# A two-layer attention and feed-forward kernel: the opening rebuilt, more doubled score matmuls, and another rule for the order of TensorE's last work

## The chip, the cores and the metric

The kernel runs on one core of one Trainium2 chip. The metric is the device time of one execution in microseconds. Every run is also profiled, and the "span" in a profile is the time from the first to the last instruction.

TensorE does the matmuls, ScalarE the exponentials, VectorE and GpSimd the rest; SyncE issues the transfers. PSUM is the memory that this kernel's matmuls write to, and an eviction is a copy out of it. The granted clock is the share of full speed at which the profile shows TensorE running. A warm-up or filler matmul is one whose result nobody reads.

## The reference

Two layers, each attention followed by a feed-forward block, both with a residual and a layer norm without gain. There are 2048 rows of 448 columns, 16 heads of 28, and a hidden width of 1792.

```python
x = A_x
x = x + attention(layernorm(x), wqkv, wo)      # softmax(q k^T / sqrt(28)) v, 16 heads
x = x + mlp(layernorm(x), w1, b1, w2, b2)      # relu(x w1 + b1)^2 w2 + b2
x = x + attention(layernorm(x), wqkv, wo)
x = x + mlp(layernorm(x), w1, b1, w2, b2)
```

## The kernel before

The kernel is a program that plans itself. While it is built, a planner keeps one clock per engine, takes the next operation from several streams (scores, exponentials, attention values, loads, one chain per block of rows) and emits it on its engine in that order. On the chip each engine then runs its own list in order.

Scores are computed transposed, three "units" of 128 keys by 512 columns to a group (32-row matmuls, four heads packed). One ScalarE exponential of 1536 columns turns a group into weights. Some units are set aside: VectorE computes their exponential by a polynomial.

```python
# every priority stream offers its next operation; the earliest start wins
s, _, e, st = min(cands, key=lambda c: (c[0], c[1]))
```

```python
# the opening: unread warm-up matmuls, emitted before anything else of TensorE
idle = ps_m[0].tile([P, QB], DT.float32, name="mt", tag="m")
for _ in range(WARM):                                  # 34
    nc.tensor.matmul(idle[:, 0:D], lhsT=b2w[:, 0:P], rhs=b2w[:, :], start=True, stop=True)
...
# loads: both halves of the first rows, then query/key weights, then value weights
yield dma(x_sb[:, 0:2, :], x_view[:, 0:2, :], 224 * kb, ("x", 0, 0))
yield dma(x_sb[:, 2:4, :], x_view[:, 2:4, :], 224 * kb, ("x", 0, 1))
yield dma(st_qk[:, 0:3, :], qk_main, 680 * kb, ("wqk", 0))
...
# the first passes take keys in four parts of 512; one pass is 4 heads of one query block
add_passes(0, [0, 1], [0, 4, 8, 12, 16])
```

```python
# doubled scores: a group is computed once or twice more in front, into the same PSUM, when TensorE
# has been busy for less than HOT of the last HWIN us and there is room before the last exponential ends
short = HOT - pl.load(HWIN) if s_left else 0.0         # HOT = 0.8
again = 0
if short > 0 and gi > 0:
    last = ("e" in gbuf[gi - 1] and gbuf[gi - 1]["e"].end) or pl.clock["ACT"] + 1.35
    again = max(0, min(MORE, int(min(o.room, last - LAT["PE"] - o.end) / 0.22)))
```

The softmax here doesn't subtract the row's maximum and nothing guards it: scores larger than these inputs give would overflow.

Of the kernel before, what the change touches and what calls it, by code (L numbers as in the profile page):

```python
# [11 lines left out]
DT = mybir.dt  # L12
AF = mybir.ActivationFunctionType
ALU = mybir.AluOpType
P = 128
H = 16
# [11 lines left out]
WARM = 34  # L28
GATE = [None, None, ('Q', 0, 0, 0), ('Q', 0, 0, 0), ('Q', 0, 2, 0), ('Q', 0, 2, 0), ('Q', 0, 2, 0), ('Q', 0, 2, 0)]
# [17 lines left out]
HOT = 0.8  # L47
# [44 lines left out]
class Planner:  # L92
# [3 lines left out]
    def __init__(self):  # L96
        self.clock = {"PE": 0.0, "ACT": 0.0, "DVE": 0.0, "POOL": 0.0, "DMA": 0.0, "-": 0.0}
        self.mode = None
        self.tok = {}
        self.streams = []  # L100
        self.past = {"PE": [], "DVE": []}

# [35 lines left out]
    def run(self):  # L138
        while self.streams:
# [14 lines left out]
            s, _, e, st = min(cands, key=lambda c: (c[0], c[1]))  # L154
# [29 lines left out]
def kernel(  # L184
# [78 lines left out]
    def dma(out_ap, in_ap, nbytes, key):  # L263
        return Op("DMA", nbytes / 230e3, lambda e: nc.sync.dma_start(out=out_ap, in_=in_ap), sets=key)

    def setup():
# [13 lines left out]
        nc.gpsimd.memset(V_sb[0][:, :, :, DH:DHP], 1.0)  # L280
        nc.gpsimd.memzero(wo[:])
        nc.gpsimd.memset(w1[DL:P, 3, :], 0.0)

        idle = ps_m[0].tile([P, QB], DT.float32, name="mt", tag="m")
        for _ in range(WARM):
            nc.tensor.matmul(idle[:, 0:D], lhsT=b2w[:, 0:P], rhs=b2w[:, :], start=True, stop=True)  # L286

    def late_setup():

        yield Op("POOL", 0.2, lambda e: nc.gpsimd.memset(sel[:], 0.0), deps=[("K", 0, 1, 3)])  # L290
# [13 lines left out]
    def loads():  # L304
        kb = 1024
        yield dma(x_sb[:, 0:2, :], x_view[:, 0:2, :], 224 * kb, ("x", 0, 0))
        yield dma(x_sb[:, 2:4, :], x_view[:, 2:4, :], 224 * kb, ("x", 0, 1))
        qk_main = A_wqkv[0:3 * P, 0:2 * D].rearrange("(c p) n -> p c n", p=P)
        yield dma(st_qk[:, 0:3, :], qk_main, 680 * kb, ("wqk", 0))
        yield dma(st_qk[0:DL, 3, :], A_wqkv[3 * P:D, 0:2 * D], 112 * kb, ("wqk",))  # L310
        v_main = A_wqkv[0:3 * P, 2 * D:3 * D].rearrange("(c p) n -> p c n", p=P)
# [6 lines left out]
        for hh in range(G):  # L318
            yield dma(wo[DHP * hh:DHP * hh + DH, :, :],
                      A_wo.rearrange("(g hh r) d -> hh r g d", hh=G, r=DH)[hh], 98 * kb, ("wo", hh))  # L320
        yield dma(w1[:, 0:3, :], B_w1[0:3 * P, :].rearrange("(c p) n -> p c n", p=P), 1344 * kb, ("w1", 0))
# [5 lines left out]
    def wprep():  # L327
# [9 lines left out]
        yield Op("ACT", 0.6, cp(wk, D, 0, 4), deps=[("wqk",)], sets=("wk", 0))  # L337
        yield Op("ACT", 0.6, cp(wq, 0, 0, 4), deps=[("wqk",)], sets=("wq", 0))
        yield Op("ACT", 1.3, cp(wk, D, 4, H), deps=[("wqk",)], sets=[("wk", g) for g in range(1, G)])
        yield Op("ACT", 1.3, cp(wq, 0, 4, H), deps=[("wqk",)], sets=[("wq", g) for g in range(1, G)])  # L340
# [27 lines left out]
    s_left = [True]  # L368

# [14 lines left out]
    def layernorm(t0, nt, deps_of, early=False, mv=None):  # L384
# [14 lines left out]
        rs = Op("POOL", 0.6, rsqrt, deps=[last])  # L399
# [11 lines left out]
        def turn(p0, own, xs):  # L411
# [17 lines left out]
            o = Op("DVE" if early else engs_now(), 0.12 + 0.3 * len(xs), ev, deps=[t], rel=t)  # L429
# [4 lines left out]
        for p0 in range(0, nt, 2):  # L434
# [4 lines left out]
            for j in js:  # L439
# [6 lines left out]
                nm = Op("DVE", 0.42, norm, deps=[rs])  # L446
# [40 lines left out]
    def copy_to(dst, by=None):  # L487
        def f(e, t):
            src = t[:, :] if len(dst.shape) == 2 else t[:, :].rearrange("p (r n) -> p r n", r=dst.shape[1])
# [10 lines left out]
    def qkv(l, t0, nt, xnT, own_xt, ends, early=False):  # L500
# [4 lines left out]
        def turned(w, dst, key, wkey, g0):  # L505
# [5 lines left out]
                copy_to(d, q_scale if key == "Q" else None), 0.70, [*ends, *[(wkey, g) for g in range(g0, g0 + r)]], True,  # L511
# [17 lines left out]
        ks = [(wk, K_sb[l], "K", "wk", g) for g in range(0, G, r)]  # L529
        qs = [(wq, Q_sb, "Q", "wq", g) for g in range(0, G, r)]  # L530
        if l == 0 and t0 == 0:
            yield from turned(*ks[0])
            yield from turned(*qs[0])
            yield from values()
            for a, b in zip(ks[1:], qs[1:]):
                yield from turned(*a)
                yield from turned(*b)
            yield Op("DVE", 0.0, None, deps=[last], rel=own_xt)
        else:
            yield from turned(*ks[0])  # L540
            yield from values()
            for a in ks[1:]:
# [454 lines left out]
```

## Time and profile before

| | before |
|---|---|
| time, median of 11 runs of one batch | 934.02 us |
| span of the profiled run | 934.9 us |
| ScalarE busy | 96%, 890.3 us of it 662 exponentials |
| first exponential starts | 15.44 us |
| waits before exponentials after 26 us | 5.46 us |
| from the end of the last exponential to the end | 21.3 us |

A line of the timeline gives start, length, engine, source line, operation, what it writes from what, and in brackets the idle time in front and who ended it. A line of the stretches gives its borders and length, the busy time of TensorE, its weight loads, VectorE, ScalarE and GpSimd with instruction counts, then the granted TensorE clock, the DMA share and GB/s. The prediction shows the main lines. Here are four stretches of one us that it does not show, where the clock falls for the first time:

```profile
99.00:100.00 1.00, 0.05 (x6) 0.01 (x3) 0.16 (x1) 1.00 (x2) 0.00 (x0) 1.00 0.00 0
100.00:101.00 1.00, 0.87 (x8) 0.30 (x8) 0.00 (x0) 1.00 (x2) 0.00 (x0) 1.00 0.00 0
101.00:102.00 1.00, 0.67 (x22) 0.46 (x24) 0.00 (x0) 1.00 (x2) 0.00 (x0) 1.00 0.00 0
102.00:103.00 1.00, 1.00 (x22) 0.41 (x14) 0.89 (x2) 1.00 (x2) 0.00 (x0) 0.55 0.00 0
```

TensorE was busy 1.59 of the 3 us before the fall (0.05 + 0.87 + 0.67), and its longest pause in them was 0.95 us. So here the clock fell without a pause of even one us.

### The profile page before, as it was taken

Reading aid. Unit: us, or ns where it says so; the run is one execution under the profiler, and the core shown is the slowest. Engines: PE = TensorE matmul, PEld = TensorE weight load, DVE = VectorE, ACT = ScalarE, POOL = GpSimd, SP = SyncE. Lnnn points to the kernel's source line nnn. Section 1 sums busy time; section 2 is a strip of 40 time slices with the busy share of each in tenths; the row PEclk is TensorE's granted clock in tenths of the full one; section 3 lists DMA queues with packets and bytes.
Section 4 is the critical chain, followed back from the end, with each engine's and each line's share of the span. In section 5 each row is a group of like instructions: output and inputs, shape, how many; then the busy total and the mean of one; then the engine's idle time right before and its main releaser. Section 6 shows DMA issues by size and latency. Waiting matters only on the chain.

```text
span 934.9 us, 28645 instructions
## 1 busy us (share of the span) xinstructions
PE 825.9 (88%) x12718; PEld 447.8 (48%) x12718; DVE 633.1 (68%) x1323; ACT 900.8 (96%) x678; POOL 41.5 (4%) x84
## 2 busy tenths in 40 slices
PE   8999878999889899999988998788989887989886
PEld 4555434454444445444454544434445444555554
DVE  6755576677776778767767656767667576576673
ACT  5999999999999999999999999999999999999992
POOL 4100000000000000000000000000000000000000
PEclk9999898999899999999999999999999999999998
DMA  9000010000000000000000000011000000000000
GB/s 274 13 2 1 2 38 19 14 9 13 14 9 13 14 8 13 13 12 4 2 2 2 1 2 2 9 37 31 24 15 16 24 17 14 20 17 24 20 11 11
DMA packets 34472, 18.40 MB, mean 20 GB/s; under 512 B 18474, under 2 KB 33899, under 8 KB 34348
## 3 DMA queue, kind: packets, MB, share of 16 engines
q1 hardware_dynamic: 34348, 16.58, 6.4%
q8 instruction: 99, 1.62, 0.7%
q14 instruction: 25, 0.20, 0.1%
HBM read 14.26 MB, written 2.07 MB: 17 GB/s over the span
## 4 chain that ended last, share of the span: by engine, by line
ACT 69%; issue 17%; PE 10%; DMA 2%; DVE 1%; SPq 0%; POOLq 0%; POOL 0%; ACTq 0%
ACT pt L668 69%; PE sc L650 3%; PE mt L476 3%; DMA dn<-oT_sb 2%; PE oT L771 1%; PE sc L476 1%; PE mt L286 1%; PE mt L951 1%; PE tp L417 0%; DVE vh L703 0%; DVE st L378 0%; DVE x_sb L866 0%; DVE oT_sb L796 0%; DVE vi L681 0%; DVE dn L838 0%
## 5 line engine op out<-in xcount | busy, mean ns | idle before, releaser
L668 ACT ACTIVATE pt<-sc 128x1536 bf16<-128x1536 f32 x662 | 890.3, 1739 | 6.3 <-PE sc L650 4.9
L650 PE MATMUL sc<-Q_sb,K_sb 32*128 32x256 bf16 (+1 forms) x5194 | 292.3, 264 | 88.7 <-ACT pt L668 84.1
L650 PEld LDWEIGHTS <-K_sb 32*128 32x128 bf16 x5361 | 131.5, 93 | 265.2 <-issue 255.3
L771 PE MATMUL oT<-pt,V_sb 128*32 128x256 bf16 (+1 forms) x4468 | 153.6, 266 | 0.6 <-ACT pt L668 0.6
L476 PE MATMUL mt<-xnT,w 128*128 128x256 bf16 (+1 forms) x968 | 122.8, 265 | 5.2 <-DVE vi L681 1.6
L771 PEld LDWEIGHTS <-V_sb 128*32 128x32 bf16 x4608 | 94.6, 97 | 45.4 <-issue 40.8
L904 DVE TENSOR_SCALAR r<-mt 128x512 bf16<-128x512 f32 x110 | 74.6, 678 | 47.1 <-PE mt L476 46.3
L476 PEld LDWEIGHTS <-w 128*128 128x128 bf16 x1008 | 82.3, 100 | 40.4 <-issue 31.4
L703 DVE SCALAR_TENSOR_TENSOR vh<-vh,vm 128x512 f32<-128x512 f32 x126 | 86.2, 684 | 1.7
L681 DVE TENSOR_SCALAR vi<-mt 128x512 int32<-128x512 f32 x63 | 43.4, 689 | 51.5 <-PE mt L650 51.1
L866 DVE TENSOR_TENSOR x_sb<-x_sb,mt 128x448 bf16<-128x448 bf16 x62 | 38.0, 613 | 40.3 <-PE mt L476 39.9
L951 PE MATMUL mt<-xn,ident 128*128 128x448 bf16 x187 | 63.1, 369 | 1.6 <-DVE xn L443 0.9
L476 PE MATMUL mt<-w,h 128*128 128x448 bf16 x224 | 53.1, 355 | 0.0
L476 PE MATMUL mt<-w,V_sb 128*128 128x448 bf16 x210 | 48.8, 354 | 0.0
L397 POOL TENSOR_TENSOR ve<-mv,eps_t 128x2 f32<-128x2 f32 (+1 forms) x34 | 9.6, 281 | 873.9 <-DVE mv L379 792.9
L708 DVE SCALAR_TENSOR_TENSOR pd<-vh,vi 128x512 bf16<-128x512 f32 x63 | 43.1, 685 | 1.7 <-PE oT L771 0.9
L703 DVE SCALAR_TENSOR_TENSOR vh<-vm 128x512 f32<-128x512 f32 x63 | 43.0, 682 | 0.0
L378 DVE BATCH_NORM_STATS2 st<-x_sb 128x6 f32<-128x448 bf16 x64 | 39.4, 616 | 1.2 <-DMA x_sb<-in_A_x_dram 0.6
L794 DVE COPY oT_sb<-oT 128x256 f32<-128x256 f32 (+1 forms) x52 | 19.7, 380 | 28.7 <-PE oT L771 28.1
L476 PE MATMUL mt<-xnT,wk 128*128 128x256 bf16 x240 | 33.1, 274 | 1.3 <-DVE V_sb L523 0.8
L443 DVE TENSOR_SCALAR xn<-x_sb,mv,rstd 128x448 bf16<-128x448 bf16 x64 | 23.5, 391 | 14.5 <-POOL rstd L398 14.1
L476 PE MATMUL mt<-xnT,wq 128*128 128x256 bf16 x240 | 33.1, 274 | 0.1
(78 smaller groups left out, 636.1 us busy)
## 6 DMA issues: line engine op xcount, KB each, us to landing
rec<-scr SPq DMA_DIRECT2D x52, 128.0 KB
x_sb<-in_A_x_dram SPq DMA_DIRECT2D x8, 224.0 KB
out_dram<-x_sb SPq DMA_DIRECT2D x16, 112.0 KB
w<-in_B_w_dram SPq DMA_DIRECT2D x1, 1568.0 KB
w<-in_B_w_dram SPq DMA_DIRECT2D x1, 1344.0 KB
dn<-oT_sb SPq DMA_DIRECT2D x52, 4.0 KB
scr<-dn SPq DMA_DIRECT2D x52, 4.0 KB
rec<-scr SPq DMA_DIRECT2D x12, 64.0 KB
```

Source lines behind the costliest of these rows:

```text
L378: nc.vector.bn_stats(out=st[:, :], in_=x_sb[:, t0 + j, :])
L443: nc.vector.tensor_scalar(out=xn[:, 0:D], in0=x_sb[:, t0 + j, :], scalar1=mv[0][:, j, 0:1], scalar2=ln["r"][:, j:j + 1], op0=ALU.subtract, ...
L476: nc.tensor.matmul(box["t"][:, c0:c0 + n], lhsT=lhsT() if callable(lhsT) else lhsT, rhs=rhs, start=a, stop=b)
L650: nc.tensor.matmul(dst[k][:, i * nt * P:(i + 1) * nt * P], lhsT=K_sb[l][rows, g, (kb + i) * P:(kb + i + 1) * P], rhs=Q_sb[rows, g, t0 * P: ...
L668: nc.scalar.activation(out=pt[:, 0:n], in_=gbuf[gi]["sc"][:, 0:n], func=AF.Exp, scale=float(np.log(2.0)) * 2.0 ** -23)
L681: nc.vector.tensor_scalar(out=box["i"][:, :], in0=src, scalar1=EXP_BIAS, scalar2=0.0, op0=ALU.add, op1=ALU.max)
L703: nc.vector.scalar_tensor_tensor(out=h[:, :], in0=src, scalar=b, in1=m, op0=ALU.add, op1=ALU.mult)
L708: nc.vector.scalar_tensor_tensor(out=pd[:, :], in0=h[:, :], scalar=b0, in1=i.bitcast(DT.float32), op0=ALU.add, op1=ALU.mult)
L771: nc.tensor.matmul(box["t"][DHP * hh:DHP * hh + DHP, 0:n], lhsT=V_sb[l][:, kb + i, 4 * g + hh, :], rhs=p[:, c0:c0 + n], start=begin and kb ...
L866: nc.vector.tensor_tensor(out=x_sb[:, tb, :], in0=x_sb[:, tb, :], in1=t[:, 0:D], op=ALU.add)
L904: nc.vector.tensor_scalar(out=r[:, 0:w], in0=t[:, 0:w], scalar1=0.0, scalar2=None, op0=ALU.max)
L951: nc.tensor.matmul(t[:, 0:D], lhsT=ident[:, :], rhs=xns[0][:, 0:D], start=True, stop=True)
```

## The change

The intent: start the stream of exponentials earlier, keep TensorE's clock up by more doubled scores, spend unread matmuls only in idle time, and let TensorE's last work go by readiness. The core of the diff, with cuts marked:

```diff
-WARM = 34
+COLD = 7.0
...
+CUT0 = (0, 2, 4, 8, 12, 16)
...
-HOT = 0.8
+HOT = 0.9
...
-            s, _, e, st = min(cands, key=lambda c: (c[0], c[1]))
+            s, _, e, st = min(cands, key=lambda c: (max(c[3][2].ready, self.clock[c[2]]) if c[2] == "PE" and self.turns() else c[0], c[1]))
...                                       # turns() is true once no scores are left to emit
+    def warm_up():                       # a stream of the lowest priority, until wk of group 0 is there
...
-        yield dma(x_sb[:, 2:4, :], x_view[:, 2:4, :], 224 * kb, ("x", 0, 1))
         yield dma(st_qk[:, 0:3, :], qk_main, 680 * kb, ("wqk", 0))
         yield dma(st_qk[0:DL, 3, :], A_wqkv[3 * P:D, 0:2 * D], 112 * kb, ("wqk",))
+        yield dma(x_sb[:, 2:4, :], x_view[:, 2:4, :], 224 * kb, ("x", 0, 1))
...                                       # wq is spread by VectorE, wk by ScalarE; three buffers are
...                                       # zeroed after the first statistics; values come last in block 0
+        gs = [(0, 1), (1, 1), (2, 2)] if early and ONE else [(g, r) for g in range(0, G, r)]
...
-    add_passes(0, [0, 1], [0, 4, 8, 12, 16])
+    for cut in zip(CUT0, CUT0[1:]):
+        if cut == (0, 2):
+            add_passes(0, [0], cut)      # first block's keys alone, first query block
+        elif cut == (2, 4):
+            add_passes(0, [0], cut)
+            add_passes(0, [1], (0, 4))
+        else:
+            add_passes(0, [0, 1], cut)
```

More of the change, by code (lines that the diff above doesn't have):

```diff
@@ L27 @@
 EXP_POLY = (37.74184817, 23.12456889, 12.30728893, -0.14556782)
-WARM = 34
-GATE = [None, None, ('Q', 0, 0, 0), ('Q', 0, 0, 0), ('Q', 0, 2, 0), ('Q', 0, 2, 0), ('Q', 0, 2, 0), ('Q', 0, 2, 0)]
+COLD = 7.0
+WQD = 1
+TURNS = 1
+ENDU = 100
+HOTE = 0.8
+WSTOP = ('wk', 0)
+XT = 1
+VEND = 1
+CUT0 = (0, 2, 4, 8, 12, 16)
+ONE = 1
+GATE = [None, None, ('Q', 0, 0, 0), ('Q', 0, 0, 0), ('s', 8), ('s', 8), ('s', 8), ('s', 8)]
 EARLY = 2
@@ L101, in __init__ @@
         self.past = {"PE": [], "DVE": []}
+        self.turns = lambda: False
     def load(self, span, eng="PE"):
@@ L261, with dma @@
     mhalf = const.tile([P, 4], DT.float32, name="mhalf")
-    def dma(out_ap, in_ap, nbytes, key):
-        return Op("DMA", nbytes / 230e3, lambda e: nc.sync.dma_start(out=out_ap, in_=in_ap), sets=key)
+    def dma(out_ap, in_ap, nbytes, key, deps=()):
+        return Op("DMA", nbytes / 230e3, lambda e: nc.sync.dma_start(out=out_ap, in_=in_ap), sets=key, deps=deps)
     def setup():
@@ L279, in setup, with junk @@
             nc.vector.memset(t[:, D:D + 1], 1.0)
-        nc.gpsimd.memset(V_sb[0][:, :, :, DH:DHP], 1.0)
-        nc.gpsimd.memzero(wo[:])
-        nc.gpsimd.memset(w1[DL:P, 3, :], 0.0)
-        idle = ps_m[0].tile([P, QB], DT.float32, name="mt", tag="m")
-        for _ in range(WARM):
-            nc.tensor.matmul(idle[:, 0:D], lhsT=b2w[:, 0:P], rhs=b2w[:, :], start=True, stop=True)
+    def warm_up():
+        box = {}
+        def junk(e):
+            if "t" not in box:
+                box["t"] = bank(first, "mt")
+            nc.tensor.matmul(box["t"][:, 0:D], lhsT=b2w[:, 0:P], rhs=b2w[:, :], start=True, stop=True)
+        first = o = Op("PE", 0.38, junk, acq=R_m)
+        yield o
+        while pl.tok.get(WSTOP) is None or pl.tok[WSTOP].end > pl.clock["PE"]:
+            o = Op("PE", 0.38 if pl.clock["PE"] < COLD else 0.19, junk)
+            yield o
+        yield Op("PE", 0.0, None, deps=[o], rel=first)
     def late_setup():
+        yield Op("POOL", 1.0, lambda e: nc.gpsimd.memset(V_sb[0][:, :, :, DH:DHP], 1.0), deps=[("rs", 2)])
+        yield Op("POOL", 0.9, lambda e: nc.gpsimd.memzero(wo[:]), sets=("wo0",))
+        yield Op("POOL", 1.6, lambda e: nc.gpsimd.memset(w1[DL:P, 3, :], 0.0), sets=("w10",))
         yield Op("POOL", 0.2, lambda e: nc.gpsimd.memset(sel[:], 0.0), deps=[("K", 0, 1, 3)])
@@ L319, in loads @@
             yield dma(wo[DHP * hh:DHP * hh + DH, :, :],
-                      A_wo.rearrange("(g hh r) d -> hh r g d", hh=G, r=DH)[hh], 98 * kb, ("wo", hh))
-        yield dma(w1[:, 0:3, :], B_w1[0:3 * P, :].rearrange("(c p) n -> p c n", p=P), 1344 * kb, ("w1", 0))
+                      A_wo.rearrange("(g hh r) d -> hh r g d", hh=G, r=DH)[hh], 98 * kb, ("wo", hh), [("wo0",)])
+        yield dma(w1[:, 0:3, :], B_w1[0:3 * P, :].rearrange("(c p) n -> p c n", p=P), 1344 * kb, ("w1", 0), [("w10",)])
         yield dma(w1[0:DL, 3, :], B_w1[3 * P:D, :], 224 * kb, ("w1", 1))
@@ L336, in cp @@
             return fn
-        yield Op("ACT", 0.6, cp(wk, D, 0, 4), deps=[("wqk",)], sets=("wk", 0))
-        yield Op("ACT", 0.6, cp(wq, 0, 0, 4), deps=[("wqk",)], sets=("wq", 0))
-        yield Op("ACT", 1.3, cp(wk, D, 4, H), deps=[("wqk",)], sets=[("wk", g) for g in range(1, G)])
-        yield Op("ACT", 1.3, cp(wq, 0, 4, H), deps=[("wqk",)], sets=[("wq", g) for g in range(1, G)])
+        for h0, h1 in ((0, 4), (4, 8), (8, H)):
+            n = (h1 - h0) * NDC * DH
+            gs = range(h0 // 4, h1 // 4)
+            yield Op("ACT", 0.2 + n / 1200, cp(wk, D, h0, h1), deps=[("wqk",)], sets=[("wk", g) for g in gs])
+            yield Op("DVE" if WQD else "ACT", 0.1 + n / (1900 if WQD else 1200), cp(wq, 0, h0, h1), deps=[("wqk",), *([("xT", 0)] if h0 and XT else [])], sets=[("wq", g) for g in gs])
     def bank(o, name):
@@ L368 @@
     s_left = [True]
+    pl.turns = lambda: TURNS == 2 or TURNS == 1 and len(s_left) == 0
     def moments():
@@ L398, in rsqrt @@
             nc.gpsimd.tensor_tensor(out=rstd[:, 0:nt], in0=ve[:, 0:nt], in1=mhalf[:, 0:nt], op=ALU.pow)
-        rs = Op("POOL", 0.6, rsqrt, deps=[last])
+        rs = Op("POOL", 0.95 if early else 0.6, rsqrt, deps=[last], sets=[("rs", t0)] if early else ())
         yield rs
@@ L428, in ev @@
                     nc.vector.tensor_copy(out=dst, in_=tp[:, :, 0:w])
-            o = Op("DVE" if early else engs_now(), 0.12 + 0.3 * len(xs), ev, deps=[t], rel=t)
+            o = Op("DVE" if early else engs_now(), 0.12 + 0.3 * len(xs), ev, deps=[t], rel=t, sets=[("xT", t0)] if early else ())
             yield o
@@ L445, in norm @@
                                             op0=ALU.subtract, op1=ALU.mult)
-                nm = Op("DVE", 0.42, norm, deps=[rs])
+                nm = Op("DVE", 0.42, norm, deps=[rs], sets=[("n", t0, j)] if early else ())
                 yield nm
@@ L488, in f @@
         def f(e, t):
-            src = t[:, :] if len(dst.shape) == 2 else t[:, :].rearrange("p (r n) -> p r n", r=dst.shape[1])
+            src = t[:, 0:dst.shape[1]] if len(dst.shape) == 2 else t[:, :].rearrange("p (r n) -> p r n", r=dst.shape[1])
             if by is not None and e == "ACT":
@@ L503, in qkv, with turned @@
         last = None
-        def turned(w, dst, key, wkey, g0):
+        def turned(w, dst, key, wkey, g0, r=r):
             nonlocal last
@@ L510, in turned @@
                  for i, g in enumerate(range(g0, g0 + r))],
-                copy_to(d, q_scale if key == "Q" else None), 0.70, [*ends, *[(wkey, g) for g in range(g0, g0 + r)]], True,
+                copy_to(d, q_scale if key == "Q" else None), 0.14 + 0.00109 * r * n, [*ends, *[(wkey, g) for g in range(g0, g0 + r)]], True,
                 [(key, l, g, tb) for g in range(g0, g0 + r) for tb in range(t0, t0 + nt)], early)
@@ L527, in values @@
                     evv, 0.62, [*ends, ("wv",), *([("s", 1)] if early else [])], True, ("V", l, tb), early)
-        ks = [(wk, K_sb[l], "K", "wk", g) for g in range(0, G, r)]
-        qs = [(wq, Q_sb, "Q", "wq", g) for g in range(0, G, r)]
+        gs = [(0, 1), (1, 1), (2, 2)] if early and ONE else [(g, r) for g in range(0, G, r)]
+        ks = [(wk, K_sb[l], "K", "wk", *g) for g in gs]
+        qs = [(wq, Q_sb, "Q", "wq", *g) for g in gs]
         if l == 0 and t0 == 0:
@@ L533, in qkv @@
             yield from turned(*qs[0])
-            yield from values()
-            for a, b in zip(ks[1:], qs[1:]):
+            for a, b in zip(ks[1:-1], qs[1:-1]):
                 yield from turned(*a)
                 yield from turned(*b)
+            if not VEND:
+                yield from values()
+            for a, b in zip(ks[-1:], qs[-1:]):
+                yield from turned(*a)
+                yield from turned(*b)
+            if VEND:
+                yield from values()
             yield Op("DVE", 0.0, None, deps=[last], rel=own_xt)
         else:
-            yield from turned(*ks[0])
+            for a in ks[:-1]:
+                yield from turned(*a)
             yield from values()
-            for a in ks[1:]:
-                yield from turned(*a)
+            yield from turned(*ks[-1])
             def queries():
@@ L556, in first_block @@
         gate = [] if GATE[blk] is None else [GATE[blk]]
-        xnT, own_xt, ends = yield from layernorm(2 * blk, 2, lambda j: [("x", blk // 2, blk % 2), *gate], early)
+        xnT, own_xt, ends = yield from layernorm(2 * blk, 2, lambda j: [("x", blk // 2, blk % 2), *gate, *([("xT", 0)] if blk == 1 and XT else [])], early)
         yield from qkv(0, 2 * blk, 2, xnT, own_xt, ends, early)
@@ L635, in fn @@
                         pl.tok["u", pi, kb] = o
-                short = HOT - pl.load(HWIN) if s_left else 0.0
+                short = (HOT if len(units) - at[0] > ENDU else HOTE) - pl.load(HWIN)
                 again = 0
@@ L960 @@
     pl.spawn(2, p_stream())
+    pl.clock["PE"] = 1.2
+    pl.clock["DMA"] = 0.9
+    pl.spawn(2.5, wprep())
     pl.spawn(3, loads())
-    pl.spawn(3, wprep())
+    pl.spawn(9.6, warm_up())
     pl.spawn(9, late_setup())
```

## The prediction

> **What bounds the kernel now.** First the page: the busy shares and the costliest group.
>
> ```profile
> PE 825.9 (88%) x12718; PEld 447.8 (48%) x12718; DVE 633.1 (68%) x1323; ACT 900.8 (96%) x678; POOL 41.5 (4%) x84
> ...
> L668 ACT ACTIVATE pt<-sc 128x1536 bf16<-128x1536 f32 x662 | 890.3, 1739 | 6.3 <-PE sc L650 4.9
> ```
>
> ScalarE is busy 96% of the span, and 890.3 of its 900.8 us are 662 exponentials. Their records overlap (mean 1739 ns), so the pitch is 890.3/662 = 1.345 us. Only 6.3 us of idle time stand directly before them. So the time is: the start of the first exponential, plus 890.3, plus whatever interrupts them, plus what follows the last one. I therefore read three stretches: the opening, the interruptions, the end.
>
> The opening, from the timeline (start, length, engine, line, what; in brackets the idle time and who ended it):
>
> ```profile
> 1.24 9.19 PE L286 MATMUL mt<-b2w 128*128 128x448 bf16 x34 [1.24 <-DVE b2w L271]
> ...
> 6.78 0.71 POOL L398 TENSOR_TENSOR rstd<-ve,mhalf 128x2 f32<-128x2 f32 x1
> ...
> 8.37 0.56 ACT L333 COPY wk<-V_sb 128x448 bf16<-128x448 bf16 x1 [6.14 <-DMA V_sb<-in_A_wqkv_dram]
> ...
> 10.58 1.05 PE L417 MATMUL tp<-ident,xn 128*128 128x128 bf16 x16
> 11.23 1.29 DVE L428 COPY xnT<-tp 128x1024 bf16<-128x1024 bf16 x2 [2.01 <-PE tp L417]
> ...
> 15.44 6.82 ACT L668 ACTIVATE pt<-sc 128x1536 bf16<-128x1536 f32 x5 [0.49 <-PE sc L650]
> ```
>
> The first exponential starts at 15.44. The rows were normalized by 9.2, but the transposes stand in TensorE's order behind 34 warm-up matmuls and begin at 10.58; then both row blocks are transposed, copied and projected in 512-column pieces before the first scores. The weights land only at 8.37.
>
> The interruptions: ScalarE's waits give 6.2 us before exponentials, in eleven waits: 0.49 is the first start, 0.24 is at 23.3 us (a further 0.40 stands before a query eviction at 25), and 5.5 lie at 107, 143, 145, 147, 242, 245, 603, 613 and 637 us. The stretches around two of these (length, busy time by engine, granted TensorE clock, DMA):
>
> ```profile
> 106.40:107.20 0.80, 0.80 (x10) 0.28 (x9) 0.80 (x2) 0.50 (x1) 0.00 (x0) 0.50 0.00 0
> 107.20:108.00 0.80, 0.80 (x10) 0.12 (x7) 0.77 (x2) 0.33 (x1) 0.00 (x0) 0.50 0.00 0
> ...
> 243.60:244.40 0.80, 0.80 (x22) 0.57 (x16) 0.00 (x0) 0.80 (x1) 0.00 (x0) 0.50 0.00 0
> 244.40:245.20 0.80, 0.80 (x19) 0.33 (x14) 0.00 (x0) 0.22 (x1) 0.00 (x0) 0.50 0.00 0
> ```
>
> The clock column says 0.50: at half speed TensorE cannot deliver scores every 1.345 us, and the fourth busy column (ScalarE) drops. At 603 it is the same; at 613 the clock had just dropped to 0.80 in the stretch before. At 637 it is 1.00, so that wait (0.77) is not a clock matter.
>
> The end: the last exponential ends at 913.63, the span at 934.9, so the tail is 21.3 us.
>
> ```profile
> 917.85 0.92 PE L476 MATMUL sc<-wo,oTn 128*128 128x448 bf16 x4
> ...
> 921.69 0.61 PE L417 MATMUL tp<-ident,xn 128*128 128x128 bf16 x4 [2.92 <-DVE xn L443]
> ...
> 922.97 1.87 PE L476 MATMUL mt<-xnT,w 128*128 128x128 bf16 x16 [0.67 <-ACT xnT L426]
> ```
>
> The last block's normalized attention output is ready at 916.5, but its output projection waits until 917.85 behind the 15 matmuls of the other block's second layer. Then TensorE idles 2.92 us and the clock falls to 0.50 from about 922 to 928, exactly where the last 56 first-layer matmuls run: the first 16 take 1.87 us where 16 of the same shape took 1.07 at 906.38.
>
> **What the Trainium skill says.** "TensorE: Matmul & The Clock Gate", Part 1 (the HAM clock gate): the array runs at half rate or full rate, decided by how busy it was in a free-running window of about 3.4 us. The trace agrees: 0.50 or 1.00, in stretches of some 3.4 to 7 us. "ScalarE: Activation LUTs", What ACT_TABLE_LOAD costs: 186 ns + 0.833 ns per column, about 93 ns of it overlapping back to back; my estimate for 1536 columns is 1372 ns, the trace has 1345, which I use. So nothing in this change can shorten one exponential. [...]1.26 MB up to the end of the query/key weights, moved at 250 then 234 then 333 GB/s from 2.0 us on, would be across at about 6.9, and the copy starts 1.4 later.
>
> **The change part by part** (the program order of the changed kernel is known, its times are not).
>
> *Opening.* The weights now go ahead of the second block's rows: 229 KB fewer in front, at some 240 GB/s 0.9 us earlier, so about 7.5. Zeroing of three buffers on GpSimd moves behind the first statistics, so the first scale is ready at about 6.0 instead of 7.5 and the first block's rows at 6.9. Only 18 warm-ups stand ahead of the transposes (14 at 0.37, 4 at 0.19 after 1.24: end at 7.2) and only 8 transposes (0.55): 7.75. VectorE copies wq of group 0 first (from 7.5, about 0.35), then the transposed rows (0.65): 8.55. Four projections of 128x256 at 0.11 for each of K, Q of group 0 and K, Q of group 1: TensorE from 8.7 to 10.6. ScalarE first has wk to spread in three copies (0.5, 0.5, 0.9, from 7.5 to 9.4), then four evictions of 256 columns (about 0.39 each, from the 0.38 of a 128x256 eviction near the end): K and Q of group 0 are there at 10.2, all four at 10.95. Scores at 10.6 plus 0.4: the first exponential at **11.0**, 4.4 earlier. Other ScalarE work between exponentials: before 0.64 + 0.53 + 0.60 = 1.77; after two of 0.60 and one of 0.39 = 1.6. Gaps: before 0.64. After, the third exponential waits for the value projection, whose PSUM buffer and eviction stand behind statistics on VectorE: I allow 1.0. The pass over keys 0 and 1 alone gives 16 units, 5.3 exponentials, some 7 us before the second block's keys are needed; by the same counting these are ready about 18, the sixth exponential wants them near 19.5. It adds four 0.4 us accumulations on VectorE, which is 68% busy: hidden.
>
> *Exponentials.* 662 again, but all of 1536 columns (before one had 1024), since one block fewer goes to VectorE (62 instead of 63): +0.4 us, 890.75.
>
> *Doubled scores.* 488 more score matmuls (5849 against 5361), i.e. about 163 repeats of three at some 0.1 us (two repeats lengthen a group from 0.40 to 0.61), 17 us of TensorE; 47 fewer filler matmuls on the identity (140 against 187) give back 9. This lies in the 88.7 us in which TensorE waits for ScalarE. I summed the nominal work of every three consecutive score groups in both programs: triples below 45% of their time fall from 22 to about 9 (rounded to tenths). The deepest before, 0.36 and 0.40, stand where the clock fell at 107 and 143. So I expect the clock dips to fall by about half, from 5.5 us of waits to 2.5.
>
> *Tail.* The order now goes by readiness: the output projection precedes the other block's second layer, whose 15 matmuls (2.8 us) fill the wait for the statistics. But that block's whole first layer (56 matmuls) now also lies at or after the last exponential, 10 of them ahead of the last denominators: -1.35 + 1.0, net -0.3 at the second block's add. With TensorE busy the clock should stay at 1.00: 56 matmuls in 56 x 0.067 = 3.75 us instead of 5.7, so -2.0. Tail **19.0**.
>
> Sum: 11.0 + 890.75 + 1.6 + 1.0 + 2.5 + 19.0 = 925.85 span. The span before (934.9) is 0.65 above the median time (934.25), so 925.2; I say **925.5**.
>
> **The rivals.** (1) The repeats stand ahead of the real scores in each group, so a heavier TensorE could become the bound: a group with two repeats has 12 matmuls of 256 columns and takes 0.61 us (0.40 with 6), plus 0.23 after the buffer is freed and 0.2 to the exponential, 1.04 of 1.345. For it: at half clock it would not fit, and whatever else TensorE has in hand when the buffer comes free delays it. Against: 103 such groups run today without a wait at full clock; there will be 160. It would take back 2 to 3 us: 928. (2) The opening gain is partly lost: VectorE carries wq, both blocks' statistics and values in strict order, and the exponentials starve between 15 and 25 us. For it: the 0.7 us I already find at the third exponential. That makes 927 to 929. (3) The dips go away entirely and the tail is as good as computed: 922 to 923. (4) The tail's VectorE order (three squares between the last projection and its add) and a clock that drops anyway eat its gain: +2, 927.5.
>
> **Range and chances.** Errors: opening 1, its gaps 1, dips 2, tail 1.5, together about 3. The rivals lean upwards. Range 921.5 to 930.5. Faster by over 2% needs 915.6 or less, more than removing every gap and dip I found; slower by over 2% needs 953. So within 2% it is, 0.97.
>
> **What would show it right or wrong.** The first exponential at 11.0 (10.5 to 12); weights landing near 7.5; waits before exponentials after 26 us of 2.5 us with a clock of 0.50 beside them; 662 exponentials at 1.345; the tail 19.0 with the clock at 1.00 in its first-layer matmuls. It is wrong if the exponentials' pitch changes, if waits at full clock appear beside twice-repeated score groups, or if ScalarE starves between 15 and 26 us by over 2 us.

## The result, and the profile after

The changed kernel took 925.89 us (median of 4 runs, 925.42 to 927.32) against 933.94 us of the kernel before beside it. The ratio is 0.9909, with a 95% interval of 0.988 to 0.9937. All ratios here are the mean time of one kernel's fast runs over that of the other's of the same rounds, so not quite the ratio of the medians quoted.

The costliest group on the page of the changed kernel:

```profile
L705 ACT ACTIVATE pt<-sc 128x1536 bf16<-128x1536 f32 x662 | 890.9, 1767 | 5.2 <-PE sc L687 5.1
```

There are 662 exponentials again, now 890.9 us, and ScalarE is busy 97% of a shorter span. The opening, from the timeline:

```profile
1.24 5.80 PE L298 MATMUL mt<-b2w 128*128 128x448 bf16 x18 [1.24 <-DVE b2w L281]
...
5.13 0.71 POOL L421 TENSOR_TENSOR rstd<-ve,mhalf 128x2 f32<-128x2 f32 x1
...
6.62 1.87 ACT L354 COPY wk<-V_sb 128x448 bf16<-128x448 bf16 x3 [4.39 <-DVE xn L466]
6.88 0.61 PE L440 MATMUL tp<-ident,xn 128*128 128x128 bf16 x8
...
7.53 0.69 DVE L451 COPY xnT<-tp 128x1024 bf16<-128x1024 bf16 x1 [0.63 <-PE tp L440]
...
10.56 1.45 ACT L705 ACTIVATE pt<-sc 128x1536 bf16<-128x1536 f32 x1
```

The first exponential starts at 10.56 instead of 15.44, and the normalized rows and the weights are now both there at 6.6. (The wait in front of the weights' copy is put down to VectorE; a second profile of the same kernel puts it down to the transfer.) Before the third exponential, at 15.13, ScalarE waits 0.79 us: the gap that the prediction allowed 1.0 for.

Waits later on, from ScalarE's timeline, and for two of them the stretch around:

```profile
132.51 254.00 ACT L705 ACTIVATE pt<-sc 128x1536 bf16<-128x1536 f32 x189 [0.97 <-PE sc L687]
...
630.38 16.31 ACT L705 ACTIVATE pt<-sc 128x1536 bf16<-128x1536 f32 x12 [1.05 <-PE sc L687]
```

```profile
387.00:388.00 1.00, 1.00 (x4) 0.30 (x2) 0.42 (x2) 1.00 (x1) 0.00 (x0) 0.50 0.00 0
...
629.00:630.00 1.00, 1.00 (x12) 0.71 (x13) 1.00 (x3) 0.33 (x1) 0.00 (x0) 1.00 0.17 34
```

There are seven waits of 4.27 us in all after 26 us. The two near 387 and those at 829 and 890 (1.91 us) stand beside a clock of 0.50; those at 132, 630 and 647 (2.36 us) stand at full clock.

The tail, from the timeline, where the last exponential ends at 908.11:

```profile
910.69 0.92 PE L499 MATMUL sc<-wo,oTn 128*128 128x448 bf16 x4
...
911.63 2.81 PE L499 MATMUL sc<-w,V_sb 128*128 128x448 bf16 x14
...
914.64 0.40 PE L440 MATMUL tp<-ident,xn 128*128 128x128 bf16 x4 [0.20 <-DVE xn L466]
...
915.71 1.05 PE L499 MATMUL mt<-xnT,w 128*128 128x128 bf16 x16 [0.67 <-ACT xnT L449]
916.60 1.95 PE L499 MATMUL sc<-xnT,w 128*128 128x128 bf16 x32
```

The output projection now stands ahead of the other block's second layer. TensorE's pause before the last transposes is 0.20 us instead of 2.92, and the 16 matmuls that took 1.87 us take 1.05. The tail is 17.1 us instead of 21.3.

In one table, the prediction's terms and two profiles of the changed kernel (us):

| term | predicted | profile | second profile |
|---|---|---|---|
| first exponential | 11.0 | 10.56 | 10.38 |
| 662 exponentials | 890.75 | 890.9 | 890.8 |
| other ScalarE work between them (measured: the rest of the span) | 1.6 | 1.4 | 1.3 |
| gaps in the opening | 1.0 | 1.02 | 1.02 |
| waits after 26 us | 2.5 | 4.27 | 2.74 |
| tail | 19.0 | 17.1 | 17.1 |
| span | 925.85 | 925.2 | 923.4 |

The sum came out, but in the first profile two terms were off by about 1.8 us each, in opposite directions; in the second only the tail was. The experiments went after those two, and after what in the opening did it.

### The profile page after: what moved, and what is told of

Read it like the earlier page. It is cut to its first block, busy times and chain, and to the rows that moved or that the text cites. A ratio compares the mean times of both kernels' runs of the same rounds, so it can differ in the third digit from the quotient of the medians.

```text
span 925.2 us, 29484 instructions
## 1 busy us (share of the span) xinstructions
PE 820.8 (89%) x13144; PEld 456.3 (49%) x13144; DVE 630.1 (68%) x1323; ACT 901.0 (97%) x681; POOL 42.5 (5%) x84
## 4 chain that ended last, share of the span: by engine, by line
ACT 70%; issue 14%; PE 8%; DMA 4%; DVE 3%; SPq 0%; POOLq 0%; POOL 0%; ACTq 0%
ACT pt L705 70%; PE mt L499 4%; DMA dn<-oT_sb 2%; PE sc L687 2%; DMA scr<-dn 1%; PE oT L808 1%; DMA rec<-scr 1%; PE sc L499 1%; PE mt L298 1%; DVE vh L740 1%; PE mt L988 0%; DVE r L941 0%; DVE x_sb L903 0%; DVE oTn L892 0%; PE tp L440 0%
## 5 line engine op out<-in xcount | busy, mean ns | idle before, releaser
L705 ACT ACTIVATE pt<-sc 128x1536 bf16<-128x1536 f32 x662 | 890.9, 1767 | 5.2 <-PE sc L687 5.1
L687 PE MATMUL sc<-Q_sb,K_sb 32*128 32x256 bf16 (+1 forms) x5649 | 303.6, 260 | 87.3 <-ACT pt L705 83.5
L687 PEld LDWEIGHTS <-K_sb 32*128 32x128 bf16 x5849 | 148.9, 92 | 256.7 <-issue 247.6
L941 DVE TENSOR_SCALAR r<-mt 128x512 bf16<-128x512 f32 (+1 forms) x108 | 73.1, 677 | 32.6 <-PE mt L499 31.2
L988 PE MATMUL mt<-xn,ident 128*128 128x448 bf16 x140 | 48.4, 358 | 1.0 <-DVE xnT L451 0.4
L499 PE MATMUL mt<-wo,oTn 128*128 128x448 bf16 x124 | 30.8, 355 | 2.8 <-DVE oT_sb L833 1.7
```

The lines of the kernel that those rows point to most:

```text
L499: nc.tensor.matmul(box["t"][:, c0:c0 + n], lhsT=lhsT() if callable(lhsT) else lhsT, rhs=rhs, start=a, stop=b)
L687: nc.tensor.matmul(dst[k][:, i * nt * P:(i + 1) * nt * P], lhsT=K_sb[l][rows, g, (kb + i) * P:(kb + i + 1) * P], rhs=Q_sb[rows, g, t0 * P: ...
L705: nc.scalar.activation(out=pt[:, 0:n], in_=gbuf[gi]["sc"][:, 0:n], func=AF.Exp, scale=float(np.log(2.0)) * 2.0 ** -23)
L941: nc.vector.tensor_scalar(out=r[:, 0:w], in0=t[:, 0:w], scalar1=0.0, scalar2=None, op0=ALU.max)
L988: nc.tensor.matmul(t[:, 0:D], lhsT=ident[:, :], rhs=xns[0][:, 0:D], start=True, stop=True)
```

## The experiments

The first batch held four kernels on one chip with one set of runs of the kernel before (934.02 us), the second likewise (935.05), the third likewise (935.05). Since waits in the middle differ from run to run, I also use the end of the last exponential less the waits after 26 us, called **net end** below. For the plan of the kernel before it is 908.2, 907.8 and 907.9 in the three profiles that have it.

### The changed kernel again

No edit.

> The changed kernel itself again, as the reference of this batch. The three parts as its own trace shows them against that of the kernel before: first exponential 4.9 us earlier, waits before exponentials after 26 us down by 1.2 us (5.5 to 4.3), tail from the last exponential's end down by 4.2 us (21.3 to 17.1), 0.6 us given back for one more full exponential. If the single profiles are typical, the time is 8 to 10 us under the kernel before. If the waits depend on where the clock's window happens to fall, the spans of the runs differ by 1 to 3 us with the mean granted clock, and the waits of a second profile are not the same ones.

It took 925.83 us, ratio 0.9909 (0.9891 to 0.9926). The spans of its five runs were 922.5 to 925.1, and their mean granted clock 0.998 to 0.988: the shortest span has the highest clock, the two longest the lowest. The waits after 26 us sum to 2.74 us, and the pair of waits near 387 is gone while another, at 276, is new. So the middle is partly a matter of chance from run to run, and a single profile's waits can't be taken for a kernel's.

### The rule for the end taken back

```diff
-TURNS = 1
+TURNS = 0
```

> Only the order at the very end goes back to the old rule; everything up to the last few score groups is the same program. Theory (the tail gains from order and clock together): the other block's 15 second-layer matmuls stand ahead of the output projection again, TensorE idles near 3 us behind it, the granted clock falls to 0.50 in the last first-layer matmuls, and the tail goes from 17.1 to 20 or 21 us: 3 to 4 us slower than the changed kernel. Rival (the tail gain comes from what the rest of the new plan left for the end, not from the rule): the tail stays within 1 us of 17.1.

It took 931.51 us, ratio 0.9967 (0.9944 to 0.9991): 5.7 us slower than the changed kernel in the same batch. The tail is 22.7 us. From its timeline:

```profile
913.65 0.92 PE L499 MATMUL mt<-wo,oTn 128*128 128x448 bf16 x4
...
917.49 0.61 PE L440 MATMUL tp<-ident,xn 128*128 128x128 bf16 x4 [2.92 <-DVE xn L466]
...
918.77 3.57 PE L499 MATMUL sc<-xnT,w 128*128 128x128 bf16 x32 [0.67 <-ACT xnT L449]
```

The pause of 2.92 us is back, and 32 matmuls take 3.57 us instead of 1.95. The expectation was 20 to 21: the direction held and the effect was larger. The rival, that the tail would stay, is out.

### The doubling threshold taken back

```diff
-HOT = 0.9
+HOT = 0.8
```

> Only the threshold for doubled scores goes back from 0.9 to 0.8; 5337 score matmuls and 188 fillers, as in the kernel before. Theory (more doubling keeps the clock up, but a part of the waits is not the clock's): waits before exponentials after 26 us rise by 1 to 2 us, more stretches at a granted clock of 0.50, mean clock 0.985 or so instead of 0.994; time 1 to 2 us longer. Rival 1 (the doubling removes most of the waits, and the profile of the changed kernel was an unlucky one): 3 to 4 us longer. Rival 2 (the doubled matmuls delay real scores as much as the clock gains): no difference, 0 plus or minus 0.5 us.

It took 930.45 us, ratio 0.9961 (0.9943 to 0.9978): 4.6 us slower than the changed kernel. Read alone, that is rival 1. But the waits after 26 us are 2.84 us, no more than before the edit, and the tail is 21.3. From its timeline:

```profile
908.26 2.81 PE L499 MATMUL sc<-w,V_sb 128*128 128x448 bf16 x14
...
910.91 0.92 PE L499 MATMUL sc<-wo,oTn 128*128 128x448 bf16 x4
```

With the new rule still on, the second layer again stands ahead of the projection. The threshold moved the plan. The other block's first layer was nearly done by the last exponential (8 matmuls left, as in the kernel before), its second layer was ready earlier than the projection, and a rule that goes by readiness let it go first. The loss sits in the tail, not in the waits that doubling was meant to cure.

### The new opening alone

```diff
-TURNS = 1
+TURNS = 0
-HOT = 0.9
+HOT = 0.8
```

> Both thresholds back: old doubling, old tail order, new opening alone. Theory (the parts add up): first exponential near 10.6 us, tail near 21 us, so some 4.5 to 5 us under the kernel before. Rival (the opening's gain is given back later, because the planned streams only shift): under 3 us below the kernel before, with more waits of ScalarE between 10 and 100 us.

It took 931.18 us, ratio 0.9963 (0.9942 to 0.9984), 2.8 us under the kernel before by the medians and 3.5 by the ratio: less than the 4.5 to 5 expected, more than the rival's by the ratio only. The rival's sign is absent: between 10 and 100 us ScalarE waits 0.79 and 0.23 us, as in the changed kernel. The first exponential starts at 10.73, the net end is 904.0 (4.2 us less than the kernel before in its profile), and the tail is 21.25. Its profile has 5.9 us of waits after 26 us. So the opening's gain reaches the last exponential.

### The tail filled, in the kernel before

13 unread matmuls are put just ahead of the last block's transposes, and nothing else:

```diff
+                if t0 == NTB - 1 and len(s_left) == 0:
+                    full = tp.rearrange("p c q -> p (c q)").bitcast(DT.float32)
+                    for _ in range(FILL):        # 13
+                        nc.tensor.matmul(full[:, 0:D], lhsT=one0[:, :], rhs=b2w[:, :], start=True, stop=True)
```

> The kernel before plus 13 unread matmuls of 448 columns (2.4 us at full clock) just ahead of the last block's transposes, where TensorE idles 2.92 us; nothing else differs. It measures the clock's share of the tail by itself. Theory (half the tail's gain is the clock): the granted clock stays at 1.00, the last 56 first-layer matmuls take 3.3 us as in the changed kernel instead of 5.7, the tail goes from 21.3 to 19.0 (18.6 to 19.4). Rival (the clock falls for another reason, or the fillers delay the transposes by as much): tail 21 or longer.

It took 932.42 us, ratio 0.9966 (0.9954 to 0.9978). The tail is 18.6 us instead of 21.3. From its timeline:

```profile
920.67 0.40 PE L422 MATMUL tp<-ident,xn 128*128 128x128 bf16 x4 [0.46 <-DVE xn L448]
921.74 1.05 PE L481 MATMUL mt<-xnT,w 128*128 128x128 bf16 x16 [0.67 <-ACT xnT L431]
```

The order is that of the kernel before, the clock stays at 1.00, and the first-layer matmuls take 1.05 us for 16. The clock alone is worth 2.7 us of the tail.

### The projection first, in the kernel before

```diff
-LASTP = 3.9
+LASTP = 3.4
```

> The kernel before with the last block's output projection given precedence over the other block's second layer: 7 of its 15 matmuls still ahead, 7 behind, not one instruction added. Theory (order gives both shares): the projection starts at 1.3 us less after the last exponential, the 7 matmuls (1.3 us) behind it shorten TensorE's idle time to about 1.6 us. If that is enough for the clock, the tail is near 18 us; if it is not, near 20. Rival (order alone gives nothing, the adds on VectorE set the pace): 21.

In the built programs 22 places of TensorE's order and 4 of VectorE's differ, all near the end, and nothing is added. It took 933.35 us, ratio 0.9982 (0.9964 to 1.0). In its profile the tail is 17.3:

```profile
916.61 0.92 PE L476 MATMUL sc<-wo,oTn 128*128 128x448 bf16 x4
...
920.44 0.40 PE L417 MATMUL tp<-ident,xn 128*128 128x128 bf16 x4 [1.59 <-DVE xn L443]
```

The projection starts 2.9 us after the last exponential instead of 4.2, and a pause of 1.59 us is left. In this run the clock stayed at 1.00, and the tail is a little under the 18 expected for that case. The time fell by 1.7 us only, and its spans vary from 928.8 to 934.9. The next run shows a part of why: the clock does not always stay up.

### The doubling threshold taken back, with the projection first

```diff
-HOT = 0.9
+HOT = 0.8
-LASTP = 3.9
+LASTP = 3.4
```

> The changed kernel with the old doubling threshold, but with the last projection given precedence, so that the tail is a good one whatever the plan left for it. It takes the two effects that were mixed in the run without doubling apart. Theory (doubling is worth little in the middle and acted on the tail through the plan): tail 17.5 to 18.5, waits before exponentials after 26 us of 3 to 5 us, time within 1.5 us of the changed kernel, 926 to 927.5. Rival (doubling is worth 3 us or more in the middle): time stays at 930 and the waits are above 6 us.

It took 926.44 us, ratio 0.9912 (0.9899 to 0.9925): the changed kernel's ratio in its own two batches is 0.9909. The projection setting alone does nothing to the changed kernel: built with it, the program is the same, instruction for instruction. So the two differ by the threshold and what the plan makes of it, and with the projection first the added doubling is worth nothing that these runs can show. From the run without doubling, this one differs in the same 22 and 4 places near the end only, and it is 0.5% faster by the ratios: the loss there was the tail's. The waits after 26 us are 2.86 us, under the 3 to 5 expected; the tail is over the 17.5 to 18.5. The tail has the same pause of 1.59 us as the run above, but here the clock fell:

```profile
912.57 0.40 PE L440 MATMUL tp<-ident,xn 128*128 128x128 bf16 x4 [1.59 <-DVE xn L466]
913.64 1.86 PE L499 MATMUL mt<-xnT,w 128*128 128x128 bf16 x16 [0.67 <-ACT xnT L449]
```

The same instructions give 1.86 us here and 1.05 there: a tail of 18.9 against 17.3.

### The reciprocals planned later

```diff
-            d1 = Op("DMA", 0.5, spread, deps=[oe], lat=0.5)
+            d1 = Op("DMA", 0.5, spread, deps=[oe], lat=1.2)
```

(and the projection first, which alone changes nothing here).

> The changed kernel planned with 0.7 us more for the small transfer of the denominators, so that their reciprocals stand later in VectorE's order. Theory (waits at full clock near 131 and 630 us come from VectorE standing before a reciprocal whose transfer has not landed, which holds up a buffer and with it the scores): VectorE's waits for that transfer fall from 14.6 us to under 6, the waits at full clock near these places go, time 0.5 to 1.5 us shorter. Rival (VectorE's waits there are harmless, or the new plan makes others): no difference or slower by up to 2 us.

It took 928.65 us, ratio 0.9934 (0.9917 to 0.9951). VectorE's waits for that transfer did fall, as these lines of its waits show, the changed kernel's first (total, times, longest):

```profile
DVE dn L875 <- DMA dn<-oT_sb: 14.6, 11, 2.5
...
DVE dn L875 <- DMA dn<-oT_sb: 5.0, 5, 1.8
```

The waits after 26 us are 3.16 us, the largest 0.67 at 812, so the 0.97 and 1.05 of the changed kernel's first profile have no counterpart. But in its second profile those two were 0.20 and 0.38 with no edit at all, and the new plan has a tail of 18.7 us. It is a miss as a gain, and by time the rival holds. The chain itself is in the changed kernel's first trace: ahead of the waits at 132 and 630 TensorE stands 1.52 and 1.57 us, each pause ended by VectorE, which had just stood 1.50 and 2.46 us for that transfer. That a later reciprocal cures this is not shown.

### Rows ahead of the weights

Only the issue order of two transfers changes; the other engines' programs are the same, line by line. (The edit is cut down to what it does.)

```diff
+            nc.sync.dma_start(out=x_sb[:, 2:4, :], in_=x_view[:, 2:4, :])   # second block's rows
             nc.sync.dma_start(out=st_qk[:, 0:3, :], in_=qk_main)            # query/key weights
```

> The changed kernel with the second block's rows issued ahead of the query/key weights again; every other engine's order is the same. Theory (the weights were the later of two arrivals, the rows' path now follows close behind them): the weights land near 8.3 instead of 6.5 us, but the copies of the transposed rows wait for the transposes until 7.5 anyway, so the first exponential is later by 1.2 to 1.5 us (11.7 to 12.0) and not by 1.8; time longer by 0.7 to 1.5 us. Rival (the load order alone makes the opening's gain): first exponential 3 us or more later.

```profile
9.00 1.87 ACT L362 COPY wk<-V_sb 128x448 bf16<-128x448 bf16 x3 [6.77 <-DMA V_sb<-in_A_wqkv_dram]
...
12.21 1.45 ACT L713 ACTIVATE pt<-sc 128x1536 bf16<-128x1536 f32 x1
```

The weights arrive at 8.9 and the first exponential starts at 12.21, 1.7 to 1.8 us later than in the two profiles of the changed kernel. That is a little more than expected, and far from the rival's 3. The net end is 906.0, some 2.3 us later. It took 928.14 us, ratio 0.9931 (0.9905 to 0.9958). Its profiled run had 7.5 us of waits after 26 us with the changed kernel's own plan, the most of all.

### Fixed warm-ups

16 more unread matmuls ahead of the first transposes, 34 in all; every other order is the same.

```diff
                 box["t"] = bank(first, "mt")
+                for _ in range(16):
+                    nc.tensor.matmul(box["t"][:, 0:D], lhsT=b2w[:, 0:P], rhs=b2w[:, :], start=True, stop=True)
```

> The changed kernel with 16 more unread warm-up matmuls put back ahead of the first transposes (34 as in the kernel before); all other orders are the same. Theory (the warm-ups were what held the transposes in the kernel before): transposes at 10.4 instead of 6.9, first exponential 3.3 to 3.6 us later (near 14), time longer by 2.5 to 3.5 us, since the 0.8 us gap before the third exponential may shrink. Rival (the weights and their copies set the start): under 1 us later.

```profile
10.43 0.61 PE L442 MATMUL tp<-ident,xn 128*128 128x128 bf16 x8
...
14.10 1.45 ACT L707 ACTIVATE pt<-sc 128x1536 bf16<-128x1536 f32 x1
```

The first exponential is 3.5 to 3.7 us later, as expected, and the net end, 907.0, is 3.3 us later. The gap of 0.79 did not shrink. By time, 927.76 us and ratio 0.9914 (0.9891 to 0.9937), it is not told apart from the changed kernel: four runs from 926.05 to 929.62 are too wide for 3 us. The profile is the measure here.

### No pass over the first block's keys alone

```diff
-CUT0 = (0, 2, 4, 8, 12, 16)
+CUT0 = (0, 4, 8, 12, 16)
```

> The changed kernel without the pass over the first block's keys alone: the second exponential already needs the second block's keys. The whole plan moves with it (58 blocks on VectorE instead of 62, one exponential more). Theory (the pass hides the second block's path from rows to keys): first exponential unchanged near 10.4, then a gap of 3 to 5 us before the second or third exponential. Rival (the second block's keys are there in time anyway): gaps before 26 us stay near 1 us. The time itself also has about 1.8 us for the four blocks more on ScalarE, and is not the measure here.

```profile
15.67 0.81 ACT L518 CAST K_sb<-sc 128x256 bf16<-128x256 f32 x2 [2.33 <-PE sc L499]
16.89 1.45 ACT L705 ACTIVATE pt<-sc 128x1536 bf16<-128x1536 f32 x1 [0.41 <-PE sc L687]
```

The first exponential starts at 10.90; the second starts at 16.89 instead of 12.89, since it needs the second block's keys: ScalarE stands 2.33 + 0.41 us and spends 0.81 on two key evictions in between. The expected 3 to 5 us of gap is 2.74 of pure waiting, a little under. It took 930.67 us, ratio 0.9957 (0.9939 to 0.9974); 892.5 - 890.8 = 1.7 us of that are two more exponentials.

### A simpler version: no added doubling, projection first, pause filled

```diff
-HOT = 0.9
+HOT = 0.8
-LASTP = 3.9
+LASTP = 3.4
+FILL = 7        # unread matmuls ahead of the last transposes, as in the filled tail above
```

> A simpler version: the new opening, the old doubling threshold, the last projection given precedence, and 7 unread matmuls in the 1.6 us in which TensorE still idles ahead of the last transposes. Theory (tail = order + clock; doubling is worth nothing in the middle): tail 17.3 with the clock at 1.00 in every run, waits of 3 to 5 us after 26 us, time 925 to 926.5, equal to the changed kernel within noise, 250 fewer doubled matmuls. Rival (the doubled scores do hold the clock up in the middle and so are needed): 2 us or more slower than the changed kernel.

```profile
911.82 0.40 PE L445 MATMUL tp<-ident,xn 128*128 128x128 bf16 x4 [0.27 <-DVE xn L471]
912.89 1.05 PE L504 MATMUL mt<-xnT,w 128*128 128x128 bf16 x16 [0.67 <-ACT xnT L454]
```

It took 924.22 us (923.48 to 924.48), ratio 0.988 (0.9866 to 0.9895), the best. The tail is 17.3, the waits after 26 us 1.82. All four runs lie within 1.0 us of each other and have a mean clock of 0.991 to 0.993. The tail is as expected; waits and time are under the 3 to 5 and the 925 to 926.5 expected, and the doubled matmuls are fewer by 512 (5849 against 5337), not by 250. It was not timed in the same batch as the changed kernel, and the intervals overlap at their edges (0.9891 to 0.9926 there), so I call it at least equal, and probably 1 to 3 us faster.

## Why the prediction was right or wrong

**The bound was read rightly.** ScalarE's exponentials set the time, their pitch did not move (890.9/662 = 1.346 us), and the rest is start, interruptions and tail.

**The opening** was right in mechanism and low by half a microsecond: 11.0 against 10.56 and 10.38. The weights' arrival was mis-sized: 0.9 us earlier was predicted from 229 KB at 240 GB/s, and about 1.8 was measured (8.3 to 6.5; 6.2 in a second profile). But that is not most of the half microsecond. In the simpler version the copies of the weights started at 7.49, as predicted, and the first exponential still stood at 10.70. Some 0.3 us lie in the steps behind the weights (there the first projection starts at 8.42, where 8.7 was predicted). With the weights at 6.6 the rows' path sets the start: the first projection begins at 8.28, directly behind the copy of the transposed rows.

By single undoing the warm-ups are worth 3.6 us and the load order 1.7, of 4.9 us in all. The two do not add, since either alone can hold up the first projection. Both together were not undone, nor were the other parts (256-column projections, query weights spread by VectorE, later zeroing), so their shares stay open. The pass over the first block's keys is worth 4 us at the second exponential. The gap before the third exponential had the right size (1.0 predicted, 0.79 measured) but another cause. The prediction put it to an eviction behind statistics on VectorE; in the trace TensorE works without a pause from 12.62, on the value projection and then the second block's transposes, until it reaches those scores at 14.69.

**The doubled scores: the step failed.** The prediction said the dips would "fall by about half, from 5.5 us of waits to 2.5" because few low triples are left. Waits after 26 us by plan, each profile once (the last column counts waits with the clock below 1 in them or in the 2 us before):

| plan | waits after 26 us | mean | mean beside a lowered clock |
|---|---|---|---|
| kernel before (3 profiles) | 5.46, 4.84, 5.77 | 5.4 | 4.6 |
| new opening, old doubling (4) | 2.84, 5.87, 2.86, 1.82 | 3.3 | 3.2 |
| new opening, more doubling (5) | 4.27, 2.74, 3.67, 7.52, 3.41 | 4.3 | 3.1 |

(The reciprocals planned later, 3.16, and the run without the first pass, 2.03, are other plans.) Between the last two rows nothing speaks for the doubling, and both scatter more than they differ. The time at half clock between 26 and 905 us is, in every profile, close to a whole number of pieces of 3.4 us: 8, 5 and 9 of them in the first row, 4, 8, 6 and 4 in the second, 3, 3, 6, 9 and 4 in the third. So one profile's waits turn largely on how many such pieces it caught. Why the first row is higher stays open: it may be the replanned middle or chance. Doubling does not keep the clock where it is needed. In the changed kernel the clock falls at 384 right behind two groups that are already doubled twice:

```profile
382.53 0.61 PE L687 MATMUL sc<-Q_sb,K_sb 32*128 32x256 bf16 x12 [0.69 <-ACT pt L705]
383.88 0.61 PE L687 MATMUL sc<-Q_sb,K_sb 32*128 32x256 bf16 x12 [0.73 <-ACT pt L705]
```

A group of 12 takes 0.61 of 1.35 us, and without other work TensorE stays near 45% busy. A threshold above 0.9 would change nothing: built with 0.95 or 1.0 and the projection first, the program is the changed kernel's, instruction for instruction (built, not run). In the planner, the room before the exponential limits the repeats. And the doubling displaced one unit from VectorE to ScalarE, the +0.4 us that the prediction had.

**The tail: both mechanisms right, the sum mis-sized, and one cause missed.** The clock was put at 2.0 us and is 2.4 in the changed kernel (56 first-layer matmuls in 3.3 us, from 915.71 to 919.0, against 5.7) plus 0.2 in the transposes ahead of them, and 2.7 when filled alone. The order was put at "net -0.3" and is -1.5: the add for the last block ends 4.3 us after the last exponential against 5.8. The step that failed is the +1.0 for the ten matmuls ahead of the denominators and the squares on VectorE. The denominators start 0.96 us after the last exponential (1.06 before), since they wait for a copy out of PSUM in any case, and the squares ran in VectorE's waits. What was missed is that the rule needs the plan: the prediction counted the other block's late first layer as a cost, but with the doubling taken back that layer is done early and the rule then changes nothing (tail 21.3). The tail's gain came from rule and threshold together, and neither the rule nor an early projection alone makes it safe while a pause of 1.59 us is left.

**The last step, from span to time,** was wrong and happened to cancel. I set the profiled span of the kernel before, 934.9, against a median of other runs and took 0.65 off. In fact time is span plus some 1.8 us in nearly every run, and that profile was among the slow ones of its kernel (spans from 929.8 to 934.9 in the later batches). With 1.8 added, the same sum would have said 927.7, against 925.9 measured: that the number came within half a microsecond is luck.

**The rivals.** The repeats did not become the bound: waits at full clock did appear, but each of the three in the first profile ends with a score group of 6 matmuls, without repeats, ahead of which TensorE stood 0.8 to 1.6 us for VectorE. Starving in the opening stayed at the 0.79 us foreseen. The tail's gain was not eaten, and the dips did not go away.

## What to carry to other kernels

When one engine's steady stream is the bound, read the time as start, stream, interruptions and tail, and price each from its own stretch; two errors of 1.8 us hid in one good sum here. In a self-planned program an edit acts through the plan as well: before a threshold is credited, look at what it moved elsewhere, and undo it with that other place held fixed. Where a short idle stretch decides the clock of what follows, fill the whole stretch: half-filled, the same last instructions gave 17.3 us of tail in one program's profile and 18.9 us in another's.

## What the Trainium skill lacked or had wrong

- "TensorE: Matmul & The Clock Gate", Why this matters for your kernels, advises against idle gaps over about 3 us. Here the clock fell without any such gap: at 102 us after 3 us with 1.59 us of work and a longest pause of 0.95, and in one profile of two after pauses of 1.59 and 0.67 us with 0.40 us of work between them. It fell at 384 us right behind twice-doubled 32-row score groups (0.61 of 1.35 us). Under "A second HAM failure mode" the page does tell of a clock that swings on short pauses between groups of matmuls, but gives no length for them. It does not say what share of its window must be busy, nor whether a matmul on 32 rows counts as one on 128 rows does; these runs put no sharp number on either. It tells of variation from run to run for the warm-up at the start; here the same program's middle varies as well, with spans of 922.5 to 925.1 us at mean clocks of 0.998 to 0.988.
- "DMA: Bandwidth & Descriptors", Anatomy of one DMA, gives about 2 us plus bytes by bandwidth for one transfer issued by GpSimd; those here are issued by SyncE. The page has no figure for what a transfer of 896-byte rows costs the one behind it. 229 KB of such rows ahead of the weights delayed them by 1.8 us between the two kernels (6.5 to 8.3), and by 2.4 to 2.7 us when only the issue order was swapped (8.9 against 6.5 and 6.2), where 240 GB/s would give 0.95. The arrival scatters: the first copy of the weights starts at 8.4 to 9.0 in the four profiles with the rows ahead, at 6.1 to 7.5 in the ten without.
